# Moving matmul operands to other starting words in a fused attention and two-layer feed-forward kernel

## The chip, the cores and the metric

The kernel runs on one core of one Trainium2 chip. The time is the device time of one execution in microseconds (us), as the median of several runs; the kernel before was timed three times. A profile is one further execution, recorded instruction by instruction.

## The reference

The reference computes, in float32, a packed attention, then a gated product, then a two-layer block. Cut to what matters:

```python
p_packed = sm_attn(p, k, v)                    # 32 packed queries against 576 keys, 8 x 8 heads
x = sm_attn(q, p_packed, p_packed)             # as a matrix: 4608 tokens x 512
x = ((x @ w1) * (x @ w2) @ w3) @ w_out         # 512 -> 1024 -> 1024 -> 512
h = x @ w_in                                   # 512 -> 2048
g = where(h >= 1, h, where(h <= -1, 0, (h + 1) ** 2 / 4))
out = g @ moe2_w_out                           # 2048 -> 512
```

## The kernel before, in words

Everything is kept with features on the partitions and tokens along the rows. A product in near-float32 precision is made of three float32r matmuls: each operand is split into a high and a low part (ScalarE copies the high part, VectorE subtracts it), and PASSES pairs high with high, high with low and low with high.

The program has three stages. The attention stage (up to about 565 us) makes the attention of the eight batches, the gated product (ab_unit, line 393) and the product with w3 @ w_out (x2_product, line 417), both with right sides of 288 columns. It stores its result to device memory. Beside it, the weights of the last two layers are combined and stored too.

The input stage is x @ w_in with the function g behind it, and the output stage is g @ moe2_w_out. Both are done by a scheme of the Strassen-Winograd kind: each operand is cut into two by two blocks, seven products (A11, S1, S2, A12, S3, S4, A22) of sums of blocks are made, and the results are combined. The tokens are taken in five pairs of blocks (PAIRS): pair 0 has two blocks of 512 tokens, pairs 1 to 4 have two of 448.

In the input stage a pair has eight steps. A step makes the seven products in function product (line 855), each of six matmuls: two pieces of the depth by three passes. The left side is a weight tile of 128 columns (wi or ws), loaded anew for every matmul; the right side is a tile x2s that has four rows of 512 words a partition (high and low part, two pieces of the depth), of which the first N words are used. All seven x2s tiles of a pair are made by x2_tasks from the tile f, which holds the pair's tokens.

In the output stage a pair has seven products of four pieces each, in function out_product (line 1036); a piece is 12 matmuls (two halves of the output features, two pieces of the depth, three passes), so a product is 48. The right side is one of five tiles op (for the first two pieces of all a tile x2s), again four rows of 512 words with the first N used; g_parts fills it. The left sides lie in three places. S1, S2, A12 and S3 take over the memory of the input stage's weights on the right end of the memory (half_tile). A11 takes the place of the tile f on the left end. S4 and A22 lie in the pool dl on the left end, ahead of the op tiles.

Tiles are laid out by pools: those on the left side follow each other from low addresses up, those on the right side from high addresses down, and a tile takes a whole number of 32 bytes in each partition. The order on the left side is: ident, half (line 76, one word, so 32 bytes), then the tiles of a2 and cv in the attention stage; later f in their place, then the pool b1 with the x2s tiles, and at the end dl in place of b1. Every tile of f, b1 and dl takes a whole number of 256 bytes, so they all begin at the same place within 256 bytes. The tiles of the attention stage that line 393 and line 417 read (at, m, g, w34) and the weights wi, ws lie on the right side.

The order of the instructions on each engine is the order in which the program is written.

Of the kernel before, what the change touches and what calls it, by code (L numbers as in the profile page):

```python
# [8 lines left out]
F32 = mybir.dt.float32  # L9
F32R = mybir.dt.float32r  # L10
# [3 lines left out]
AF = mybir.ActivationFunctionType  # L14
ALU = mybir.AluOpType
# [7 lines left out]
P = 128  # L23
# [7 lines left out]
PAIRS = [(0, 512), (1024, 448), (1920, 448), (2816, 448), (3712, 448)]  # L31
# [20 lines left out]

TAIL = ['u7', 'x0', 'b2', 'x1', 'x2', 'b3', 'x3', 'm2', 'x4', 'm3', 'b4', 'x5', 'v0', 'b5', 'x6', 'v1', 'b6', 'v2', 'x7', 'b7', 'v3', 'v4', 'b8', 'v5', 'v6', 'v7', 'y0', 't0', 'y1', 'y2', 'n1', 'n0', 'y3', 'b9', 'y4', 'y5', 'n3', 'n2', 't1', 'y6', 'y7']
SCALE = 1.0 / 8.0

PASSES = ((0, 0), (0, 1), (1, 0))

# [2 lines left out]
def fused_kernel(ctx: ExitStack, tc, qT, kT, vv, pb, w1, w2, w3T, wo, win, wout, out):  # L60
    nc = tc.nc
# [11 lines left out]
    tmp = ctx.enter_context(tc.tile_pool(name="tmp", bufs=1, side="left"))  # L73
    ident = tmp.tile([P, P], F32, name="ident")
    make_identity(nc, ident)
    half = tmp.tile([P, 1], F32, name="half")
    nc.vector.memset(half, 0.5)

    t1 = tc.alloc_tile_pool(name="t1", bufs=1, side="right", reuse_waits="tile")
# [100 lines left out]
    def small(n, name):  # L180
        return a2.tile([P, n], F32, name=name, tag=name, bufs=2)
# [11 lines left out]
    def attention(b, joint=False):  # L193
# [3 lines left out]
        def scores_k(G):  # L197
# [6 lines left out]
            def ew():  # L204
                mx = small(1, "mx")
                nc.vector.tensor_reduce(out=mx, in_=c["ps"][:, :, :HS], axis=AX.XY, op=ALU.max)
                nb = small(1, "nb")
                nc.vector.tensor_scalar(out=nb, in0=mx, scalar1=-SCALE, scalar2=None, op0=ALU.mult)
                if G == 0:
# [4 lines left out]
                    out=e.rearrange("p (a n) -> p a n", a=2), in_=c["ps"][:, :, :HS], func=AF.Exp,  # L214
                    scale=SCALE, bias=nb, accum_out=c["sum"][:, G:G + 1],
                )
# [66 lines left out]
        def scores_q(hf):  # L283
# [10 lines left out]
            def ew():  # L294
# [8 lines left out]
                c["l", hf] = l  # L303
                exp = lambda: nc.scalar.activation(out=l, in_=l, func=AF.Exp, scale=SCALE)
                if b:
# [52 lines left out]
    def emit(step):  # L358
        pe, ew = step
        if pe:  # L360
            pe()
        ew()

    def together(*steps):
        def pe():
            for p, _ in steps:
                p()

        def ew():
            for _, e in steps:  # L370
                e()
        return pe, ew
# [4 lines left out]
    late = {}  # L377
# [232 lines left out]
    def flush_weights(age=1):  # L610
        w_stores[:] = [(n - age, f) for n, f in w_stores]
        while w_stores and w_stores[0][0] <= 0:
            w_stores.pop(0)[1]()
# [81 lines left out]
    x2f = {}  # L695
    x2_t = {}

    def x2_load(t):
        t0, N = PAIRS[t]
        f = late["f"].tile([P, 4, 1024], F32, name="f", tag="f", bufs=1)  # L700
        nc.sync.dma_start(out=f[:, :, :2 * N], in_=x2d[0][:, :, t0:t0 + 2 * N])
        for r in range(2):
            for c in range(2):
                x2f[10 * r + c + 11] = f[:, 2 * r:2 * r + 2, c * N:(c + 1) * N]

    def x2_tasks(t):

        N = PAIRS[t][1]

        def combine(dst, a, b):  # L710
            return lambda: nc.vector.tensor_tensor(out=x2f[dst], in0=x2f[a], in1=x2f[b], op=ALU.subtract)

        def parts(q, src):
            def f():
                x = x2_t[t, q] = late["b1"].tile([P, 2, 2, 512], F32R, name="x2s", tag="x2s", bufs=9)
                nc.scalar.activation(out=x[:, 0, :, :N], in_=x2f[src], func=AF.Copy)
                nc.vector.tensor_tensor(
                    out=x[:, 1, :, :N], in0=x2f[src], in1=x[:, 0, :, :N].bitcast(F32), op=ALU.subtract)
            return f
        return [  # L720
            parts(A11, 11), combine(11, 12, 11), combine(12, 22, 12), parts(S1, 11), combine(11, 22, 11),
            parts(S2, 11), parts(A12, 21), parts(S4, 22), parts(S3, 12), combine(11, 21, 11), parts(A22, 11),
        ]

    for b in range(1, B):
        if b + 1 < B:
            att, sa, bm = attention(b + 1, True)
            spread = dict(zip(EARLY, att))
            spread.update(zip(LATE, [together(bm[1, 0], bm[0, 0]), *sa, together(bm[1, 1], bm[0, 1])]))
        else:  # L730
            spread = {}
            late["f"] = tc.alloc_tile_pool(name="fp", bufs=1, side="left", reuse_waits="tile")
            b1 = late["b1"] = tc.alloc_tile_pool(name="b1", bufs=1, side="left", reuse_waits="tile")
            x2_load(0)
            x2_todo = x2_tasks(0)
        seq = []
        for f, n in ((ab_unit, 8), (x2_unit, 4)):
            seq += [f(b, mt, hf) for hf in range(2) for mt in range(n)]
        for u, unit in enumerate(seq):
            emit(unit)  # L740
            if u in spread:
                emit(spread[u])
            if b == B - 1:
                if (u > 3 and u % 3 < 2) and x2_todo:
                    x2_todo.pop(0)()
                    if not x2_todo:
                        x2_load(1)
            else:
                flush_weights()
                for _ in range(WORK[u]):  # L750
                    task = w_todo.pop(0) if w_todo else None
                    if task:
                        task()
        if b == B - 2:
            flush_weights(2)
            cv.release()
            a2.release()
# [78 lines left out]
    def psb(b):  # L836
        return first.pop(b) if b in first else psB.tile([P, 512], F32, name=b, tag=b, bufs=BUFS[b])

    bank = {}

    def product(s, q):
        t, i = divmod(s, 8)
        N = PAIRS[t][1]
        b = BANK[q]
        if q in (A11, S1, A12):
            bank[s, b] = psb(b)
        n, c0 = divmod(i, 4)
        j = 0
        for k in range(2):
            for v, m in PASSES:  # L850
                if q in STREAM:
                    w = ws_t[s, STREAM.index(q)][:, k, v, :]
                else:
                    w = wi_t[q, n][:, c0, k, v, :]
                nc.tensor.matmul(  # L855
                    bank[s, b][:, :N], w, x2_t[t, q][:, m, k, :N],
                    start=(j == 0 and q in (A11, S1, A12)), stop=(j == 5), skip_group_check=True,
                )
                j += 1
# [85 lines left out]
    seq = [(t, q, j) for t in range(len(PAIRS)) for q in order for j in range(4)]  # L945
    w2_t, rawg, op = {}, {}, {}
    RAWS, OPS = 6, 5
# [8 lines left out]
    def w2_tile(q, pool, tag):  # L956
        w = pool.tile([P, 4, 1024], F32R, name=f"w2{q}", tag=tag, bufs=1)
        w2_t[q] = [w[:, 2 * x:2 * x + 2].rearrange("p a (b n) -> p (a b) n", n=256).rearrange(
            "p (k v) n -> p k v n", v=2) for x in range(2)]
# [27 lines left out]
    def op_tile(n):  # L987
        return ring("op", n, [P, 2, 2, 512], F32R)
# [21 lines left out]

    def g_parts(x):
        if x < len(seq):
            N = PAIRS[seq[x][0]][1]
            if x < 2:
                o = op[x] = late["b1"].tile([P, 2, 2, 512], F32R, name="x2s", tag="x2s", bufs=9)
            else:
                o = op[x] = op_tile(x % OPS)
            a = rawg.pop(x)
            count[2] -= len(a)
            nc.scalar.activation(out=o[:, :, 0, :N], in_=a[0], func=AF.Copy)  # L1020
            nc.vector.tensor_tensor(  # L1021
                out=o[:, :, 1, :N], in0=a[0], in1=o[:, :, 0, :N].bitcast(F32), op=ALU.subtract)

    def out_product(x):
        t, q, j = seq[x]
        N = PAIRS[t][1]
        b = BANK[q]
        start = j == 0 and q in (A11, S1, A12)  # L1030
        if start:
            bank[b] = [psb(b) for _ in range(2)]
        for d in range(2):
            for k in range(2):
                for n, (s, v) in enumerate(PASSES):
                    nc.tensor.matmul(  # L1036
                        bank[b][d][:, :N], w2_t[q][j // 2][:, 2 * (j % 2) + k, s, d * P:(d + 1) * P], op[x][:, k, v, :N],
                        start=start and k == 0 and n == 0, stop=(j == 3 and k == 1 and n == 2), skip_group_check=True,
                    )

# [33 lines left out]
    for s in range(steps):  # L1074
        t, i = divmod(s, 8)
        N = PAIRS[t][1]
# [25 lines left out]
        if s + 1 == steps:  # L1102
            g_parts(1)
            g_load(6)
# [25 lines left out]
    dl = late["op"] = tc.alloc_tile_pool(name="dl", bufs=1, side="left", reuse_waits="tile")  # L1130
    for q in (S4, A22):
        w2_tile(q, dl, f"w2{q}")
    for n in range(OPS):
        tiles["op", n] = op_tile(n)
    g_parts(2)
# [114 lines left out]
```

## Time and profile before

| | us |
|---|---|
| median of 3 runs | 1262.63 |
| lowest and highest run | 1262.03, 1264.18 |
| profiled execution | 1263.47 |
| its span, first to last instruction | 1261.7 |
| TensorE busy in the span | 1247.9 |
| VectorE busy | 842.1 |
| ScalarE busy | 695.2 |

The profiled execution's own time is 1.8 us over its span. Matmuls are pipelined: each record lasts longer than the time until the next one starts, and busy time counts the time in which at least one is under way. The mean length of one matmul is therefore not what it costs in a queue; that is read from the start of one to the start of a later one, and the chain of work gives it for groups. An x and a number is how many instructions a row stands for.

### The profile page before, as it was taken

The page shows a single profiled execution, that of the slowest core. Times are in us where ns is not written, and L with a number is a line of the kernel's source. Part 1 is how long each engine was busy: PE and PEld are TensorE (multiplying, and loading weights), DVE is VectorE, ACT ScalarE, POOL GpSimd, SP SyncE. Part 2 cuts the span into 40 slices and gives each one's busy share as a digit, 9 for nine tenths or more (in the row PEclk, how much of TensorE's full clock was granted, in tenths as well). Part 3 has the DMA queues.
Part 4 walks back from the last instruction along what each step waited for, and adds up shares of the span by engine and source line. Part 5 has one row for each costly group of instructions (what it writes and reads, how often), then busy time and mean ns, then how long its engine had stood idle before and what let it go on. Part 6 is the DMA issues. An engine that isn't in the chain of part 4 may idle for free.

```text
span 1261.7 us, 21619 instructions
## 1 busy us (share of the span) xinstructions
PE 1247.9 (99%) x8344; PEld 1100.7 (87%) x8344; DVE 842.1 (67%) x1356; ACT 695.2 (55%) x1184; POOL 47.0 (4%) x86
## 2 busy tenths in 40 slices
PE   8999999999999999999999999999999999999998
PEld 4468899999999899998889999999978999999997
DVE  3675787857677776717788788786768555554545
ACT  5774546544546454526676767776764534444342
POOL 0000100001010101010000000000000000000000
PEclk9999999999999999999999999999999999999999
DMA  8872566636656533279776776768999778586855
GB/s 313 317 279 85 168 227 207 232 138 224 194 191 231 192 125 114 81 256 371 256 272 237 247 263 224 274 212 292 357 353 383 249 237 277 195 276 223 295 185 170
DMA packets 137415, 297.12 MB, mean 235 GB/s; under 512 B 11104, under 2 KB 93216, under 8 KB 133472
## 3 DMA queue, kind: packets, MB, share of 16 engines
q1 hardware_dynamic: 104896, 241.73, 54.5%
q10 hardware_dynamic: 27424, 36.97, 8.9%
q0 software_dynamic: 4992, 17.04, 4.1%
q8 instruction: 65, 1.06, 0.4%
q14 instruction: 38, 0.31, 0.1%
HBM read 195.04 MB, written 100.66 MB: 234 GB/s over the span
## 4 chain that ended last, share of the span: by engine, by line
PE 85%; DMA 8%; ACT 3%; DVE 2%; issue 1%; SPq 0%; ACTq 0%; DVEq 0%
PE psk L393 16%; PE psk L417 15%; PE x L1036 15%; PE x L855 11%; PE z L1036 7%; PE z L855 6%; PE y L1036 4%; PE y L855 3%; PE psk L186 3%; PE psk L521 2%; DMA g<-L 2%; DMA wi<-wi 2%; PE psm L186 1%; DMA raw<-wo 1%; DMA raw<-w 1%; DMA r<-g 1%
## 5 line engine op out<-in xcount | busy, mean ns | idle before, releaser
L393 PE MATMUL psk<-at,m 128*128 128x288 f32 x1536 | 216.4, 298 | 0.0
L417 PEld LDWEIGHTS psk<-g,w 128*128 128x128 f32 x1536 | 204.8, 188 | 12.7 <-ACT m L107 10.1
L393 PEld LDWEIGHTS psk<-at,m 128*128 128x128 f32 x1536 | 205.6, 188 | 11.3 <-issue 5.1
L417 PE MATMUL psk<-g,w 128*128 128x288 f32 x1536 | 210.2, 296 | 0.0
L855 PE MATMUL x<-x2s,wi 128*128 128x448 f32 (+1 forms) x720 | 162.2, 369 | 1.6 <-ACT m L928 1.6
L855 PEld LDWEIGHTS x<-x2s,wi 128*128 128x128 f32 x720 | 134.2, 188 | 17.4 <-ACT m L928 4.0
L1021 DVE TENSOR_TENSOR op<-raw,op 128x896 fp32r<-128x896 f32 (+1 forms) x93 | 100.3, 1114 | 72.4 <-ACT op L1020 71.8
L1020 ACT ACTIVATE op<-raw 128x896 fp32r<-128x896 f32 (+1 forms) x93 | 86.7, 967 | 67.5 <-DVE raw L1009 39.8
L1036 PE MATMUL x<-op,hwi 128*128 128x448 f32 (+1 forms) x480 | 100.7, 368 | 0.2 <-DVE op L1021 0.2
L1036 PEld LDWEIGHTS x<-op,hwi 128*128 128x128 f32 x480 | 89.9, 188 | 9.3 <-DVE op L1021 0.6
L1036 PE MATMUL x<-op,w 128*128 128x448 f32 (+1 forms) x456 | 96.5, 371 | 0.0
L1036 PEld LDWEIGHTS x<-op,w 128*128 128x128 f32 x456 | 85.6, 188 | 9.9
L405 DVE TENSOR_TENSOR tb<-psk,ta 128x288 f32<-128x288 f32 x128 | 57.9, 453 | 51.8 <-ACT ta L403 24.1
L866 ACT ACTIVATE r<-r 128x896 f32<-128x896 f32 (+1 forms) x80 | 78.0, 975 | 2.5
L1021 DVE TENSOR_TENSOR op<-r,op 128x896 fp32r<-128x896 f32 (+1 forms) x45 | 48.6, 1107 | 39.3 <-ACT op L1020 39.2
L403 ACT ACTIVATE ta<-psk 128x288 f32<-128x288 f32 x128 | 51.7, 406 | 37.3 <-PE psk L393 37.1
L869 DVE SCALAR_TENSOR_TENSOR U<-U,r 128x448 f32<-128x448 f32 (+1 forms) x80 | 47.4, 633 | 32.5 <-ACT r L866 32.5
L928 ACT ACTIVATE m<-x 128x448 f32<-128x448 f32 (+1 forms) x40 | 22.1, 552 | 82.8 <-PE x L855 52.6
L108 DVE TENSOR_TENSOR m<-psk,m 128x512 fp32r<-128x512 f32 x62 | 38.6, 683 | 39.9 <-ACT m L107 39.9
L128 ACT ACTIVATE cvt<-raw 128x512 f32<-128x512 f32 (+1 forms) x74 | 49.1, 663 | 25.5 <-DMA raw<-w3T 8.6
L1020 ACT ACTIVATE op<-r 128x896 fp32r<-128x896 f32 (+1 forms) x45 | 42.1, 962 | 36.1 <-DVE r L1009 18.9
L521 PE MATMUL psk<-wo,w3f 128*128 128x512 f32 x128 | 57.6, 599 | 3.3 <-DVE w3f L141 2.9
(123 smaller groups left out, 1929.0 us busy)
## 6 DMA issues: line engine op xcount, KB each, us to landing
raw<-g SPq DMA_DIRECT2D x84, 448.0 KB, 4.5
g<-L SPq DMA_DIRECT2D x64, 448.0 KB, 3.5
r<-g SPq DMA_DIRECT2D x44, 448.0 KB, 4.7
g<-U SPq DMA_DIRECT2D x64, 224.0 KB, 3.5
raw<-g SPq DMA_DIRECT2D x24, 512.0 KB, 6.7
ws<-ws SPq DMA_DIRECT2D x42, 256.0 KB, 4.3
v<-vv SPq DMA_DIRECT2D x8, 1280.0 KB, 7.4
wi<-hl ACTq DMA_DIRECT2D x20, 512.0 KB, 4.4
```

The lines of the kernel that those rows point to most:

```text
L128: nc.scalar.activation(out=t, in_=words.bitcast(F32)[:, :, 1], func=AF.Prelu, scale=2.0 ** -112, alpha=2.0 ** 32)
L186: nc.tensor.matmul(ps[r][NP * q:NP * q + NP], stat[64 * r:64 * r + 64, NP * q:NP * q + NP], mov(q)[64 * r:64 * r + 64], start=True, stop=True,
L393: nc.tensor.matmul(ps[w][:, :HS], m_tile[b, w, n][:, s, G, c0 * P:(c0 + 1) * P], at_tile[b][:, G, v, hf * HS:(hf + 1) * HS], start=(k == 0 ...
L403: nc.scalar.activation(out=bs, in_=ps[1][:, :HS], func=AF.Copy)
L405: nc.vector.tensor_tensor(out=g, in0=ps[0][:, :HS], in1=bs, op=ALU.mult)
L417: nc.tensor.matmul(ps, w34[kt][:, s, mt * P:(mt + 1) * P], g_t[kt, hf][:, v, :], start=(kt == kts[0] and n == 0), stop=(kt == kts[-1] and ...
L521: nc.tensor.matmul(acc[4 * hf + m], w3f[hf, j][:, m * P:(m + 1) * P], wof[j], start=(j == 0), stop=(j == 7))
L855: nc.tensor.matmul(bank[s, b][:, :N], w, x2_t[t, q][:, m, k, :N], start=(j == 0 and q in (A11, S1, A12)), stop=(j == 5), skip_group_check= ...
L866: nc.scalar.activation(out=r, in_=r, func=AF.Square)
L1020: nc.scalar.activation(out=o[:, :, 0, :N], in_=a[0], func=AF.Copy)
L1021: nc.vector.tensor_tensor(out=o[:, :, 1, :N], in0=a[0], in1=o[:, :, 0, :N].bitcast(F32), op=ALU.subtract)
L1036: nc.tensor.matmul(bank[b][d][:, :N], w2_t[q][j // 2][:, 2 * (j % 2) + k, s, d * P:(d + 1) * P], op[x][:, k, v, :N], start=start and k == ...
```

## The change

Three things are changed, and nothing else. The tile half grows from 1 word to 56 words (of which the first is used as before), so it takes 224 bytes in place of 32. A tile edge of 16 words is put into the pool b1 ahead of the x2s tiles, and another into the pool dl behind S4 and A22 and ahead of the op tiles. And the N words that a right side uses no longer begin at word 0 of each row of 512, but at a word that depends on the pair: XOFF gives it for the x2s tiles of the input stage, GOFF for the right sides of the output stage. For pair 0 both are 0. The instructions on each engine, their order and the semaphores that they wait for are the same as before, row for row; what differs is the addresses.

```diff
 SCALE = 1.0 / 8.0
+XOFF = (0, 16, 8, 56, 24)
+GOFF = (0, 40, 8, 56, 16)
+EDGE = 56
...
-    half = tmp.tile([P, 1], F32, name="half")
+    half = tmp.tile([P, EDGE], F32, name="half")[:, :1]
     nc.vector.memset(half, 0.5)
...
         def parts(q, src):
             def f():
-                x = x2_t[t, q] = late["b1"].tile([P, 2, 2, 512], F32R, name="x2s", tag="x2s", bufs=9)
-                nc.scalar.activation(out=x[:, 0, :, :N], in_=x2f[src], func=AF.Copy)
-                nc.vector.tensor_tensor(
-                    out=x[:, 1, :, :N], in0=x2f[src], in1=x[:, 0, :, :N].bitcast(F32), op=ALU.subtract)
+                x = late["b1"].tile([P, 2, 2, 512], F32R, name="x2s", tag="x2s", bufs=9)
+                x = x2_t[t, q] = x[:, :, :, XOFF[t]:XOFF[t] + N]
+                nc.scalar.activation(out=x[:, 0], in_=x2f[src], func=AF.Copy)
+                nc.vector.tensor_tensor(out=x[:, 1], in0=x2f[src], in1=x[:, 0].bitcast(F32), op=ALU.subtract)
             return f
...
             b1 = late["b1"] = tc.alloc_tile_pool(name="b1", bufs=1, side="left", reuse_waits="tile")
+            b1.tile([P, 16], F32, name="edge", tag="edge", bufs=1)
...
                 nc.tensor.matmul(
-                    bank[s, b][:, :N], w, x2_t[t, q][:, m, k, :N],
+                    bank[s, b][:, :N], w, x2_t[t, q][:, m, k],
                     start=(j == 0 and q in (A11, S1, A12)), stop=(j == 5), skip_group_check=True,
                 )
...
     def g_parts(x):
         if x < len(seq):
-            N = PAIRS[seq[x][0]][1]
+            t, _, _ = seq[x]
+            N = PAIRS[t][1]
             if x < 2:
-                o = op[x] = late["b1"].tile([P, 2, 2, 512], F32R, name="x2s", tag="x2s", bufs=9)
+                o = late["b1"].tile([P, 2, 2, 512], F32R, name="x2s", tag="x2s", bufs=9)
             else:
-                o = op[x] = op_tile(x % OPS)
+                o = op_tile(x % OPS)
+            o = op[x] = o[:, :, :, GOFF[t]:GOFF[t] + N]
             a = rawg.pop(x)
             count[2] -= len(a)
-            nc.scalar.activation(out=o[:, :, 0, :N], in_=a[0], func=AF.Copy)
-            nc.vector.tensor_tensor(
-                out=o[:, :, 1, :N], in0=a[0], in1=o[:, :, 0, :N].bitcast(F32), op=ALU.subtract)
+            nc.scalar.activation(out=o[:, :, 0], in_=a[0], func=AF.Copy)
+            nc.vector.tensor_tensor(out=o[:, :, 1], in0=a[0], in1=o[:, :, 0].bitcast(F32), op=ALU.subtract)
...
     for q in (S4, A22):
         w2_tile(q, dl, f"w2{q}")
+    dl.tile([P, 16], F32, name="edge", tag="edge", bufs=1)
     for n in range(OPS):
         tiles["op", n] = op_tile(n)
```

## Rows read from the trace of the kernel before

**Rows 1.** The page: span, and busy time of each engine with its share.
```profile
span 1261.7 us, 21619 instructions
PE 1247.9 (99%) x8344; PEld 1100.7 (87%) x8344; DVE 842.1 (67%) x1356; ACT 695.2 (55%) x1184; POOL 47.0 (4%) x86
```
**Rows 2.** The page: chain that ended last, share of the span by engine.
```profile
PE 85%; DMA 8%; ACT 3%; DVE 2%; issue 1%; SPq 0%; ACTq 0%; DVEq 0%
```
**Rows 3.** Cores: span, mean granted TensorE clock (1 is full).
```profile
core 0: 1261.7 us, clock 0.999
```
**Rows 4.** Waits of PE, whole span: us in total, times, longest us.
```profile
PE psk L521 <- DVE w3f L141: 2.9, 2, 1.5
PE x L855 <- ACT m L928: 1.6, 4, 0.7
```
**Rows 5.** Chain in order of time, output stage: start us, us, engine, bank, line.
```profile
952.24 10.99 PE x L1036 x48
963.23 10.88 PE z L1036 x48
974.11 20.61 PE x L1036 x96
994.72 9.61 PE z L1036 x48
1004.33 9.60 PE x L1036 x48
1013.93 9.60 PE y L1036 x48
1023.53 9.60 PE x L1036 x48
1033.13 9.92 PE z L1036 x48
1043.05 19.84 PE x L1036 x96
...
1237.63 9.92 PE z L1036 x48
1247.55 9.93 PE x L1036 x48
```
**Rows 6.** The same chain, cut to 703 to 790 us, input stage.
```profile
719.58 1.20 PE z L855 x6
720.78 2.40 PE x L855 x12
723.18 1.20 PE y L855 x6
```
**Rows 7.** The same chain, cut to 504 to 550 us, end of the attention stage.
```profile
504.59 25.44 PE psk L393 x192
```
**Rows 8.** Stages: from:to, length, then each engine's busy us, clock, DMA share, GB/s.
```profile
703.80:712.20 8.40, 8.08 (x41) 7.24 (x40) 8.33 (x13) 5.58 (x10) 0.00 (x0) 1.00 0.57 189
738.20:746.60 8.40, 8.40 (x43) 7.88 (x43) 7.04 (x11) 6.28 (x10) 0.00 (x0) 1.00 0.72 250
...
995.00:1261.70 266.70, 262.46 (x1295) 242.51 (x1293) 139.44 (x146) 110.02 (x137) 8.59 (x12) 1.00 0.68 228
```

More of the change, by code (lines that the diff above doesn't have):

```diff
@@ L1036, in out_product @@
                     nc.tensor.matmul(
-                        bank[b][d][:, :N], w2_t[q][j // 2][:, 2 * (j % 2) + k, s, d * P:(d + 1) * P], op[x][:, k, v, :N],
+                        bank[b][d][:, :N], w2_t[q][j // 2][:, 2 * (j % 2) + k, s, d * P:(d + 1) * P], op[x][:, k, v],
                         start=start and k == 0 and n == 0, stop=(j == 3 and k == 1 and n == 2), skip_group_check=True,
```

## The prediction

> **What bounds the kernel now.** I read the page's shares first, then its chain, then the chain in order of time, piece by piece, then the waits, then the stages. TensorE (PE) is busy for 99% of the span and VectorE for 67%, and the chain that ended last is 85% PE [rows 1, 2]. [...] PE's longest waits on another engine are 2.9 and 1.6 us in total [rows 4]. So the last two thirds of the span are a queue of matmuls with hardly a hole in it, and what counts is how long one matmul keeps the next from starting.
>
> That is not one number. In the output stage each product of one pair is 48 matmuls, and the chain gives it as one piece [rows 5]. For 448 columns S1, S2, A12 and S3 take 9.60 us each, 200.0 ns a matmul. S4 takes 9.92 us, A22 of one pair together with A11 of the next 19.84 us for 96: 206.7 ns. Nothing else differs: the same number of columns, the same right-hand tiles, the same engine never waiting. In the input stage six matmuls of 448 columns take 1.20 us, 200.0 ns again [rows 6]. For 512 columns the order is the other way round: 10.99 us for S3 of pair 0 and 10.88 us for S4, 229.0 and 226.7 ns [rows 5].
>
> [...]
>
> What differs is where the operands lie. Count a tile's first byte modulo 256, in eighths of 32 bytes, from the tiles' sizes: before, all right sides (x2s, op) start at eighth 5. The left sides of S1, S2, A12 and S3, and all of the input stage, start at eighth 3. Those of A11 (in the place of f), S4 and A22 (pool dl) start at eighth 5, where the right sides start too. The weight load of the next matmul runs beside the current one, so the two operands are read at the same time. My reading is that equal starts make them meet once more.
>
> **The change, part by part.** No instruction is added, taken away or moved, and no wait changes: addresses alone do. So all terms are "so many matmuls times a difference in ns", and these are on the path wherever PE is.
>
> *The tile half, 56 words for one.* It takes 224 bytes for 32, so everything behind it on the left side moves by 192 bytes, six eighths. A11's, S4's and A22's left sides go from eighth 5 to 3, where the other four are. The tile edge, 64 bytes, brings the right sides to 256 bytes in all, so eighth 5 stays for offset 0. If the place decides, the three products cost what the other four cost. From the rows: S4 four times 0.32 us, the three double pieces 0.64 each, the last A22 0.33, and the first A11 0.13 (20.61 less 10.88 for A22 of pair 0 leaves 9.73): 1.28 + 1.92 + 0.33 + 0.13 = 3.66 us saved [rows 5]. In pair 0 the same rule makes S4 and A22 dearer by 0.11 us each; with as much for A11, 0.3 us lost. Net 3.3 us saved. From both sides: nothing if the place isn't the cause; 4.0 us would be all of it without the loss in pair 0.
>
> *Operands of the attention stage.* qk, v, et and pp move by the same six eighths, but the two costly lines of that stage read tiles of the right side, which stay; they run at 132.5 ns for 288 columns [rows 7]. I put these moves at 0, within 1 us either way.
>
> *The starts of the right sides, pair by pair.* XOFF moves x2s by 16, 8, 56 and 24 words, GOFF moves op by 40, 8, 56 and 16. From eighth 5 the input side gets to 7, 6, 4 and 0, the output side to 2, 6, 4 and 7. Eight groups of 336 matmuls (8 steps of 42, or 7 products of 48), 2688 together. No row shows 448 columns at any of these starts, so each is bounded by the step on either side: 6.67 ns less (206.7 to 200.0 taken once more downwards) or 6.67 ns more (200.0 to 206.7). For all eight groups that is 17.9 us down or up. [...] So I take 0 in the sum, which treats the present 13.3 as typical, and keep both ends.
>
> *ScalarE and VectorE* now write x2s and op at these starts. In the output stage they are busy 110.0 and 139.4 of 266.7 us, so that is covered [rows 8]. In the input stage VectorE has 7.04 of 8.40 us in an ordinary step but 8.33 in the last step of a pair [rows 8]: there a slower write would show, and there a faster PE would gain nothing. That caps a large gain by about 1 us in four pairs, and costs nothing otherwise.
>
> *Sum.* Profiled execution 1263.47 us (span 1261.7 and 1.8 around it), less 3.3: 1260.2. The median of the runs is 0.84 lower, 1262.63, and on it the forecast is 1259.3 us.
>
> [...]
>
> **The rivals.**
>
> *Whole blocks of 64 bytes.* If the row is read in blocks of 64 bytes, 448 columns at an odd eighth touch 29 blocks and at an even one 28. Six of the eight groups come to even eighths (6, 4, 0 and 2, 6, 4). That saves one step in 6 x 336 matmuls: 13.4 us, with the 3.3 1245.9 us, or about 1247 with VectorE's limit. [...]
>
> [...]
>
> *The place isn't the cause.* A11, S4 and A22 also lie in the low part of the memory with the right sides, the other four at its high end. If nearness in that sense makes the 6.67 ns, 192 bytes change nothing, and neither do the offsets: 1262.6 us. For it: with 512 columns the same equal starts are the cheaper ones. [...]
>
> **How the numbers follow.** My case, three products to 9.60 us and the right sides about level, 0.42; its own range is 1256.6 to 1262.0, for a mean of 1 ns either way over 2688 matmuls. Whole blocks, in full or in part, 0.22. The meeting, 0.22. No effect of place, 0.14. A measurement of this kernel can tell about 0.2%, 2.5 us, from no change. My case is faster in three quarters of its range, the whole blocks are faster always: 0.54. The rest of my case, the case without effect, and a few meetings that just eat the gain: 0.24 within. Most of the meeting: 0.22 slower. The range of eight in ten leaves out the full block gain and the worst of the meeting: 1249 to 1267.
>
> **What would show it.** In the chain of the changed kernel S4, A22 and A11 of pairs 1 to 4 should stand with the same length as the other four products of their pair; if they are still 0.32 longer, the place of the left sides isn't the cause. In pair 0 A22 should be 10.99 and not 10.88. Each group should show its own ns: 1.20 us for six in the input stage and 9.60 for 48 in the output stage where the start costs nothing, 1.16 and 9.28 where a step goes, 1.24 and 9.92 where one is added. Were the even eighths all at 9.28, the block rival holds; were odd and even mixed, it is a matter of distance. If one offset on both sides (8 and 56 words are used in both stages) gave different ns, the place of the right side alone would not decide. The forecast is wrong if the eight groups don't cancel.

## The result and the profile after

The changed kernel is slower: 1269.93 us (median of 6 runs, 1267.74 to 1270.54) against 1262.89 before, a ratio of 1.0055 with a 95% interval of 1.0043 to 1.0068. The forecast was 1259.3 in a range of 1249 to 1267. The profiled execution took 1270.23 us at the same granted clock, 0.999.

PE is as full as before; its instructions only start further apart. On the page, the span, the busy times and the chain by engine, which answer to [rows 1, 2]:

```profile
span 1268.5 us, 21619 instructions
PE 1255.9 (99%) x8344; PEld 1101.4 (87%) x8344; DVE 842.2 (66%) x1356; ACT 694.8 (55%) x1184; POOL 47.0 (4%) x86
...
PE 86%; DMA 9%; ACT 3%; DVE 1%; issue 1%; SPq 0%; ACTq 0%; DVEq 0%
```

The chain in order of time in the output stage, which answers to [rows 5] (start us, us, engine, bank, line; out_product is now line 1041):

```profile
966.61 10.99 PE z L1041 x48
...
998.39 9.81 PE z L1041 x48
...
1037.65 9.81 PE z L1041 x48
...
1067.12 9.86 PE z L1041 x48
...
1106.55 9.86 PE z L1041 x48
...
1136.18 9.92 PE z L1041 x48
...
1175.86 9.92 PE z L1041 x48
...
1205.48 9.80 PE z L1041 x48
...
1244.65 9.79 PE z L1041 x48
```

The first row is S4 of pair 0; of each of pairs 1 to 4 stand S1 (the first z) and S4 (the second). Two things are to be seen. S4 is now as long as S1 in every pair: the 0.32 us between them are gone. And no pair has 9.60 any more: 9.81, 9.86, 9.92 and 9.80, which are 204.4, 205.3, 206.7 and 204.0 ns a matmul from one start to the next, over a whole pair.

The input stage shows the same by pair. The same chain, cut to four undisturbed stretches, one in each of pairs 1 to 4, which answers to [rows 6] (product is now line 859):

```profile
690.22 1.23 PE y L859 x6
691.44 1.22 PE z L859 x6
...
734.96 1.23 PE z L859 x6
...
803.32 1.24 PE y L859 x6
...
877.34 1.20 PE z L859 x6
```

Over a whole stretch these are 204.0 ns from start to start at 16 words, 205.3 at 8, 206.7 at 56 and 200.0 at 24. What both stages have in common agrees: 8 words give 205.3 in both, 56 words 206.7, 16 words 204.0.

Against the spans, 6.8 us longer: the output stage's pairs 1 to 4 take 3.2 us more (6.9 lost by the right sides, 3.7 won by the left sides) and the input stage's 3.9 more. The rest lies ahead of these pairs: the input stage starts 0.7 later, and pair 0 of the output stage takes 1.0 less, though three of its products became 0.11 dearer each, so that its waits became shorter. In the input stage the slower matmuls took part of their loss out of waits that PE's weight loads had before: waits of PEld from 640 to 915 us (us in total, times, longest), of the kernel before and then of the changed one:

```profile
PEld x L855 <- ACT m L928: 4.0, 7, 1.1
PEld x L855 <- DVE L L932: 1.0, 2, 0.5
```
```profile
PEld x L859 <- ACT m L932: 3.3, 7, 0.9
PEld x L859 <- DVE L L936: 0.4, 1, 0.4
```

That is 1.3 us less waiting, out of the 5.4 that 336 x (4.0 + 5.3 + 6.7 + 0) ns would have cost.

### The profile page after: what moved, and what is told of

It reads as the page before. It is cut to its first block, busy times and chain, and to the rows that moved or that the text cites. A ratio compares the mean times of both kernels' runs of the same rounds, so it can differ in the third digit from the quotient of the medians.

```text
span 1268.5 us, 21619 instructions
## 1 busy us (share of the span) xinstructions
PE 1255.9 (99%) x8344; PEld 1101.4 (87%) x8344; DVE 842.2 (66%) x1356; ACT 694.8 (55%) x1184; POOL 47.0 (4%) x86
## 4 chain that ended last, share of the span: by engine, by line
PE 86%; DMA 9%; ACT 3%; DVE 1%; issue 1%; SPq 0%; ACTq 0%; DVEq 0%
PE psk L396 16%; PE psk L420 15%; PE x L1041 15%; PE x L859 13%; PE z L1041 7%; PE z L859 7%; PE y L1041 4%; PE y L859 3%; PE psk L189 3%; DMA raw<-w3T 2%; DMA wi<-wi 2%; DMA raw<-w 1%; DMA g<-L 1%; PE psm L189 1%; DMA raw<-wo 1%; DMA r<-g 1%
```

## The experiments

Below, "distance" is the first byte of the right side less that of the left side, modulo 256 bytes, in eighths of 32 bytes. All ns are from the start of one matmul to the start of the next, as the chain's pieces or the single starts in the trace give them.

### Part one alone

```diff
-XOFF = (0, 16, 8, 56, 24)
-GOFF = (0, 40, 8, 56, 16)
+XOFF = (0, 0, 0, 0, 0)
+GOFF = (0, 0, 0, 0, 0)
```

> Part one alone: half and the edge tiles as in the change, all right sides at word 0 again. Places are counted modulo 256 bytes in eighths of 32. Theory A (what counts is the distance, right side's first byte less left side's, here 2 eighths everywhere): every product of 48 matmuls of 448 columns takes 9.60 us in the chain, six in the input stage 1.20 us, the products of pair 0 10.99 us; time 1262.9 - 3.3 = 1259.6 us. Theory B (only the right side's own place counts, and S4, A22 and A11 were dearer for another reason): S4 stays at 9.92 and the double pieces at 19.84 us; time 1262.9 us.

Measured: 1259.14 us (9 runs) against 1262.12, ratio 0.9978 (0.9968 to 0.9987). The chain in the output stage, S4 of pair 1 with A22 and the next A11, and the end of pair 4:

```profile
1031.90 9.60 PE z L1041 x48
1041.50 19.20 PE x L1041 x96
...
1233.50 9.60 PE z L1041 x48
1243.10 9.62 PE x L1041 x48
```

Every product of pairs 1 to 4 is at 9.60, as theory A said to the hundredth, and the time fell by 3.0 us where 3.3 was worked out. The left sides' part of the forecast is shown; theory B is out.

### Part two alone

```diff
-EDGE = 56
+EDGE = 1
...
-            b1.tile([P, 16], F32, name="edge", tag="edge", bufs=1)
...
-    dl.tile([P, 16], F32, name="edge", tag="edge", bufs=1)
```

> Part two alone: the offsets of the right sides as in the change, half of one word and no edge tiles, so S4, A22 and A11 have left sides at eighth 5 again. Both theories: input stage as in the change (204.2, 205.3, 206.7, 200.0 ns in pairs 1 to 4), and S1, S2, A12, S3 at 9.81, 9.86, 9.92, 9.80 us. Theory A, from what the same distances cost so far: S4 and A22 at distances 5, 1, 7 and 2, so 9.60, 9.92, 9.81 and 9.60 us in pairs 1 to 4; time about 1.7 us under the change's, 1268.2. Theory B: S4 and A22 like the other four of their pair, 9.81, 9.86, 9.92, 9.80 us; time as the change's, 1269.9.

Measured: 1267.89 us (4 runs) against 1262.12, ratio 1.0041 (1.0025 to 1.0056). The chain, S3 and S4 of pairs 1 to 4 (here x, then z, each time):

```profile
1026.96 9.81 PE x L1040 x48
1036.77 9.60 PE z L1040 x48
...
1095.45 9.86 PE x L1040 x48
1105.31 9.92 PE z L1040 x48
...
1164.40 9.81 PE x L1040 x48
1174.21 9.81 PE z L1040 x48
...
1232.82 9.80 PE x L1040 x48
1242.62 9.60 PE z L1040 x48
```

All four S4 came out at what their distance had cost elsewhere: 9.60, 9.92, 9.81, 9.60. With right sides that start at the same word, moving the left side alone turns 9.81 into 9.60 in pair 1 and 9.86 into 9.92 in pair 2. So neither operand's own place sets the time by itself, and the distance told it in all four S4. It doesn't tell everything: S1, S2, A12 and S3 of pair 3, at distance 1, took 9.81 each and not the 9.92 that both theories had, while S4 of pair 2 took 9.92 at the same distance in the same run.

### The other distances

```diff
+XOFF = (0, 32, 48, 4, 12)
+GOFF = (0, 64, 20, 28, 36)
```

> The change with other offsets: x2s by 32, 48, 4 and 12 words in pairs 1 to 4, right sides of the output stage by 64, 20, 28 and 36. Distances right less left: input stage 6, 0, 2.5 and 3.5 eighths, output stage 2 (once round the 256 bytes), 4.5, 5.5 and 6.5. Theory A: the second input pair, distance 0, costs 206.7 ns a matmul as S4 did before (1.24 us for six); the first output pair, a whole 256 bytes on, 9.60 us for 48 as at offset 0; distance 6 and the halves are unknown, between 200.0 and 206.7. Theory B: right side at eighth 3 is unknown, and nothing ties it to 206.7; the first output pair 9.60 us only if the period is 256 bytes. If smaller units than 32 bytes count, the halves lie off the line between their neighbours.

Measured (one run): 1268.2 us. The chain in the output stage, a product of pair 0 and of each of pairs 1 to 4:

```profile
942.21 11.20 PE y L1041 x48
...
1017.24 9.60 PE y L1041 x48
...
1085.38 9.92 PE y L1041 x48
...
1154.45 9.80 PE y L1041 x48
...
1223.02 9.79 PE y L1041 x48
```

64 words, a whole 256 bytes, cost what 0 costs: 9.60, so the period holds in the one row that tests it. Units of 16 bytes made a difference, as far as one execution tells: distance 2.5 costs 203.3 ns, where 2 has 200.0 and 3 has 205.3, and 4.5 costs 206.7, where 4 has 204.0. The input stage gave 202.2 at distance 6, 202.7 at 0, 203.3 at 2.5 and 206.7 at 3.5. Distance 0 was not the 206.7 that theory A had from S4. And pair 0, with the addresses of part one alone, took 11.20 us a product, 233.3 ns, where that run had 10.99.

### Half and a quarter of the weight load

```diff
-                        bank[b][d][:, :N], w2_t[q][j // 2][:, 2 * (j % 2) + k, s, d * P:(d + 1) * P], op[x][:, k, v],
+                        bank[b][d][:M, :N], w2_t[q][j // 2][:, 2 * (j % 2) + k, s, d * P:d * P + M], op[x][:, k, v],
```

with M 64, or 32, in passes 1 and 2, and 128 in pass 0.

> The change, but in the output stage two of the three passes load and use only 64 of the 128 left columns (half of the weight load's bytes; the low-order corrections of the other 64 output rows are left out). The number and the place of the right-hand reads are the same. Theory A (the two reads meet): fewer meetings, the products of pairs 1 to 4 fall from 9.81 to 9.92 us to 9.3 to 9.7. Theory B (the right side's own read is slow at such places): 9.81, 9.86, 9.92 and 9.80 us as in the change. The input stage is as in the change by both.

> As the run with half of the weight load, but with 32 of 128 columns in two of the three passes of the output stage (the low-order corrections of the other 96 output rows are left out). If the bytes of the load take the time: below 9.74, 9.81, 9.71 and 9.81 us in pairs 1 to 4, to 9.5 to 9.7. [...]

Measured (one run each): 1267.54 and 1269.56 us. The chain, a product of pair 1 and one of pair 3, first with 64 columns, then with 32:

```profile
1017.22 9.74 PE y L1042 x48
...
1154.00 9.71 PE y L1042 x48
```
```profile
1019.47 9.71 PE y L1042 x48
...
1155.87 9.74 PE y L1042 x48
```

Pairs 1 to 4 go from 9.81, 9.86, 9.92 and 9.80 to 9.74, 9.81, 9.71 and 9.81, and to 9.71, 9.76, 9.74 and 9.81: at most 0.21 us of 9.92, and not in the order of the bytes. None came to the 9.3 to 9.7 us that theory A had, though 9.71 is close. The loads themselves did become shorter: a record of 188 ns at 128 columns, 134 or 135 at 64, 108 at 32. Pair 0 became dearer with the quarter, 11.20. So theory A's picture, two reads that meet and pay for each meeting, isn't borne out: with a third and then half of the load's bytes gone pair 4 won nothing (9.80, then 9.81 twice), and pair 3 won less with half gone (9.74) than with a third (9.71). Whether the place of the load's first bytes is enough by itself, these two runs don't tell.

A row beside the point mattered more. In the run with 64 columns the input stage has the addresses of the change, and in pair 3, at distance 1, the chain shows two values in one pair:

```profile
799.63 1.20 PE z L859 x6
800.83 2.48 PE x L859 x12
803.32 1.24 PE y L859 x6
```

200.0 ns a matmul up to 801.7 us, 206.7 after it. Distance is not the whole of it. The weight loads of the same trace show what stands between: one that waited 0.16 us for VectorE (start us, us, engine, line, what; in brackets the idle time before).

```profile
800.47 1.19 PEld L859 LDWEIGHTS x<-x2s,wi 128*128 128x128 f32 x6
801.82 0.70 PEld L859 LDWEIGHTS x<-x2s,ws 128*128 128x128 f32 x4 [0.16 <-DVE L L936]
```

The first six matmuls of the chain's middle row still run at 200.0; the row is 2.48 us long because the wait is in it.

This holds wider. In the traces of the change and of all runs with the whole weight load, and in the input stages of the two with part of it, a queue of 448 columns without a pause never left its value while the distance stayed, past the first few matmuls at that distance and over up to 1344. At an unchanged distance the value changed at a pause of the queue alone: at distance 1 from 204.4 to 206.7 (the change itself, early in pair 3 of the input stage, and two other runs), from 206.7 to 200.0 (twice) and here from 200.0 to 206.7, at distance 0 from 206.7 to 202.7. Most pauses change nothing: distances 2, 3 and 4 came out of each at 200.0, 205.3 and 204.0.

### A state that is carried on

Pair 0 of the output stage had shown 229.0 and 233.3 ns at the same addresses. Here the addresses are those of part one alone, but for the input pair that runs last ahead of it, which is at distance 3.5:

```diff
+XOFF = (0, 0, 0, 0, 12)
+GOFF = (0, 0, 0, 0, 0)
```

> Part one alone, and x2s of the last input pair begin 12 words on (distance 3.5). With the same addresses in pair 0 of the output stage as in part one alone, the run with other offsets had 11.20 us a product (233.3 ns) and not 10.99. Theory: a state is carried from product to product, and that last input pair set it: pair 0 of the output stage at 11.20 us, pairs 1 to 4 back at 9.60. Rival: something else in that run did it, such as the waits at the stage's start: 10.99 us. Input pair 4 at 206.7 ns by both.

Measured (one run): 1261.83 us. The chain in the output stage, a product of pair 0 and one of pair 1:

```profile
942.21 11.20 PE y L1041 x48
...
1015.82 9.60 PE y L1041 x48
```

11.20 again. Distance 2 with 512 columns had two values, 229.0 and 233.3 ns, and both runs with an input pair at 206.7 right ahead had the second. That this pair set it fits, but isn't shown: one execution of each kernel was profiled, and the second value also comes without such a pair. The run with other offsets had 233.3 ns at the start of the input stage, from 559 to 567 us, before any matmul of 448 columns, and 229.0 after that, though no pause stands between. Pair 1 is at 9.60 all the same, so what is carried, if anything is, wasn't seen with its 448 columns.

### Does a pair keep the value that it is entered with?

```diff
+XOFF = (0, 0, 56, 0, 8)
+GOFF = (0, 0, 56, 0, 8)
```

> Part one alone, but pair 2 begins 56 words on in both stages (distance 1) and pair 4 8 words on (distance 3); pairs 0, 1 and 3 stay at distance 2, so each is entered from a queue at 200.0 ns. Theory: at 448 columns the distance alone sets the value: 206.7 ns in pair 2 (9.92 us for 48, 1.24 for six), 205.3 in pair 4 (9.86 and 1.23), 9.60 and 1.20 in the others. Rival: the state that is carried in sets it, so a pair entered from 200.0 ns keeps it until something breaks the queue: 9.60 in pair 2 of the output stage, where nothing does, and 9.60 or a value of its own in pair 4.

Measured (one run): 1264.77 us. The chain, a product of pair 2 and one of pair 4 of the output stage, and before them a piece of pair 2 of the input stage:

```profile
737.12 1.20 PE z L859 x6
...
1082.88 9.92 PE y L1041 x48
...
1219.33 9.86 PE y L1041 x48
```

In the output stage each pair took the value that its distance had in the change, 206.7 and 205.3, out of a queue that ran at 200.0: nothing is simply kept. But in the input stage of the same run distance 1 ran at 200.0, where the change had 206.7: it began at 206.7 there too, and came out of a pause at 713 us at 200.0. So distance 1 had 200.0 and 206.7 in one input stage, and the value changed at a pause.

### The other low distance

24 words, distance 5, was the one new start at 200.0 in the change. Here all pairs of 448 columns have it:

```diff
+XOFF = (0, 24, 24, 24, 24)
+GOFF = (0, 24, 24, 24, 24)
```

> The change with 24 words for pairs 1 to 4 in both stages: right sides at eighth 0, distance 5, which so far was seen at 200.0 ns in the input stage's last pair and in S4 and A22 of one pair. Distance theory: all of pairs 1 to 4 at 9.60 and 1.20 us, pair 0 at 10.99; time as part one alone, 1259.1 us against 1262.6 before. Block rival: a whole 64-byte start is a block of 6.67 ns less than an odd one: 9.28 us, about 1241. If the low value belonged to eighth 5 of the right side, 9.81 to 9.92 and 1268 or more.

Measured: ten runs in two groups, at a granted clock of 0.998 to 1.0 in all of them: 1257.65, 1257.89, 1259.77, 1260.88, and six from 1268.59 to 1270.16. The ratio, 1.0014 (0.9986 to 1.0042), is a mean over both groups and says little. The profiled execution is one of the upper group. Its chain, a piece of the last pair of the input stage and a product of pair 1 of the output stage:

```profile
877.53 1.20 PE y L859 x6
...
1006.23 9.92 PE x L1041 x48
```

The input stage ran at 200.0 and the whole output stage at 206.7, at one distance. 1344 matmuls by 6.67 ns are 9.0 us, about the gap between the groups. That the lower group had 200.0 in the output stage is argued from that gap and not shown, since no execution of that group was profiled. All three expectations missed this. One thing it shows: no product reached 9.28, though distance 5 puts the right sides at a multiple of 64 bytes, so the block rival has no row left.

### 288 columns

The last row that the forecast leaned on was the attention stage's, 132.5 ns a matmul [rows 7]. Here its right sides begin 8 words further in each batch, on top of part one alone:

```diff
-                    at_tile[b] = a1.tile([P, 2, 2, S], F32R, name="at", tag="at", bufs=1)
+                    at_tile[b] = a1.tile([P, 4 * S + 64], F32R, name="at", tag="at", bufs=1)[
+                        :, 8 * b:8 * b + 4 * S].rearrange("p (g v n) -> p g v n", g=2, v=2)
```

> Part one alone, and in the attention stage the right side at of line 393 (396 here) begins 8 words further in each batch b: distances b eighths for the first half of the tokens, b + 4 for the second. 288 columns. Distance theory: batch 0 as before, 131.7 ns at distance 0 and 133.3 at 4; the other batches differ from each other, between 130 and 140 ns, and batches b and b + 4 show the same two values the other way round. If at 288 columns the weight load sets the time and not the place: 131.7 to 133.3 in all batches.

Measured (one run): 1260.96 us. By distance, over all batches, the matmuls of 288 columns took 131.7 to 132.0 ns at 0, 2 and 3 and 133.0 to 133.4 at 1, 4, 5, 6 and 7; batches four apart, which have the same two distances, agree to 0.4 ns. The last batch, at 7 and 3, takes in the chain what it took before at 4 and 0 [rows 7]:

```profile
505.00 25.44 PE psk L397 x192
```

So place counts here too, but 1.7 ns lie between the ends, against 6.7 at 448 columns, and there is nothing to be had.

### The version that the runs point to

Distance 2 is the only one that showed nothing but 200.0 with 448 columns, out of every pause too, and distance 0 has the lowest value seen with 512, 226.7 (at distance 2 it was 229.0 or 233.3). So: the left sides moved, no edge tiles, 16 words in pairs 1 to 4 and none in pair 0.

```diff
-            b1.tile([P, 16], F32, name="edge", tag="edge", bufs=1)
...
-    dl.tile([P, 16], F32, name="edge", tag="edge", bufs=1)
...
+XOFF = (0, 16, 16, 16, 16)
+GOFF = (0, 16, 16, 16, 16)
```

> Left sides moved, no edge tiles, all offsets 16 words for pairs 1 to 4 and 0 for pair 0: distance 0 for 512 columns (226.7 ns in S4 of pair 0 before), distance 2 for 448 (200.0 ns). Distance theory: pair 0's products 10.88 us for 48, its undisturbed input steps 9.52 us, all of pairs 1 to 4 at 9.60 and 1.20; against part one alone 672 matmuls by 2.3 ns less, 1259.1 - 1.5 = 1257.6 us. If what went before decides as much as the distance: pair 0 at 10.99 us or over, and 1259 or more.

Measured: 1259.11 us (5 runs, 1257.19 to 1259.75) against 1262.77, ratio 0.9964 (0.9950 to 0.9977). The chain in the output stage, pair 0's last products and one of pair 1:

```profile
963.18 10.88 PE z L1040 x48
974.06 20.49 PE x L1040 x96
...
1013.75 9.60 PE y L1040 x48
```

Pair 0 is at 10.88 and the others at 9.60, as the distances said. By time it is faster than the kernel before, and so than the changed one; the 1257.6 that was worked out was missed by 1.5 us. Against part one alone (0.9978) the intervals overlap: what it has over that one is shown by the rows and not by the times.

## Why the prediction was wrong

*What bounds the kernel, and what one matmul costs:* held. The whole result is matmuls that start further apart at the same clock (0.999 before and after), in the same order.

*The tile half:* held. S4, A22 and A11 came down to the other products of their pair, and alone it gave 3.0 us where 3.3 were worked out. (The bound for it without the loss in pair 0 is the sum itself, 3.7 us and not 4.0.)

*ScalarE and VectorE, and the operands of the attention stage:* held at nothing; the waits for both that PE's weight loads had from 640 to 915 us became shorter, 3.7 us for 5.0.

*The starts of the right sides, pair by pair:* this is the step that failed. "So I take 0 in the sum, which treats the present 13.3 as typical". It was not typical, it was the least. No run shows the 13.3, meant as the part of the 200.0 ns that goes beyond the columns: what the traces show is the whole time from one start to the next, 200.0 ns in most products before and 200.0 to 206.7 ns in the eight groups. Over 200.0 ns the eight groups cost 4.0, 5.3, 6.7 and 0.0 in the input stage and 4.4, 5.3, 6.7 and 4.0 in the output stage, 4.6 in the mean. By 336 matmuls each that is 12.3 us; the traces of the change and of part one alone differ by 10.7 in these pairs, and 1.3 of the rest is waiting that went away. Less the 3.0 us that the left sides gave, that is 7.7, against the 7.0 by which the median rose.

Two readings led to it. The bounds were laid evenly on both sides, though no row of 448 columns stood under 200.0 ns: with a lowest value that most products share and a few dearer ones, the profile spoke for a floor, and a blind move from a floor can only lose. And the row that was taken for the nearest, 288 columns at 132.5 ns, was a false neighbour: with 288 columns all eight distances lay within 1.7 ns, so it told nothing of 448. It was also a mean of two: in the trace of before, 131.6 ns at distance 0 and 133.3 at 4. A lesser slip moved only the chances: about two thirds of the range that the prediction gives its own case lie 2.5 us or more under 1262.6, not three quarters.

Of the other cases, *the meeting*, with a chance of 0.22, had the sign and nearly the size. By it some new starts cost 6.67 ns a matmul more, 2.24 us a group, and with four of the eight groups that is 1262.6 - 3.3 + 9.0 = 1268.3 us. It came by seven of eight groups at 4.0 to 6.7 ns, so that the nearness of 1268.3 to 1269.9 is in part luck; a price for each meeting of the right side's read with the weight load is not what the smaller loads showed. *Whole blocks* is out: even eighths came to 200.0 to 206.7 ns in the change, and nothing was under 200.0. *The place isn't the cause* is out by part one alone, where S4 went from 9.92 to 9.60. In part two alone 9.81 became 9.60 in pair 1 with the left side alone at another place.

What stays open is the mechanism. Seen at 448 columns, in ns from start to start, by distance in eighths:

```
0    202.7, 206.7          3    205.3         5.5  204.2
1    200.0, 204.4, 206.7   3.5  206.7         6    202.2
2    200.0                 4    204.0         6.5  204.0
2.5  203.3                 4.5  206.7         7    204.4
                           5    200.0, 206.7
```

All lie from 200.0 to 206.7 ns, within one step of 6.67 ns. Distances 2.5, 4.5, 5.5, 6 and 6.5 were each seen in one execution. Which values a distance allows, and what picks among them, no run tells. That the distance alone doesn't pick is shown by both values within one pair of the input stage, and the traces show when a value changes at 448 columns: with the distance, or at a pause. Why a pause brings the one or the other, whether a state was carried into pair 0 of the output stage, and what parts the two groups of one program's times stay open.

## What to carry to other kernels

Where PE is full (99% of the span here), read what one matmul costs from start to start, product by product, and compare those of equal shape. Here a step between them, 206.7 against 200.0 ns, was a matter of where the two operands lie to each other, and moving the left sides of three products by 192 bytes won 3.0 us back. Leave operands alone that stand at the lowest value the trace has (200.0 ns here; seven of eight groups that were moved off it lost 4.0 to 6.7 ns a matmul), and when no row shows a lower one, put the bounds of a blind shift on the side of a loss. Time such a kernel several times and look behind each pause: at distance 5 one program had 200.0 ns in its input stage and 206.7 in its output stage, and its runs lay in two groups about 9 us apart.

## What was not expected

One program, at a granted clock of 0.998 to 1.0, had two times: 1257.7 to 1260.9 and 1268.6 to 1270.2 us, with every pair of 448 columns at distance 5. And 16 bytes made a difference: 203.3 ns at distance 2.5 against 200.0 at 2, and 206.7 at 4.5 against 204.0 at 4, each half seen in one execution.
